# Moving norm steps and tile additions from VectorE to GpSimd in a two-layer transformer kernel

## The chip, the cores and the metric

The kernel runs on one core of a Trainium2 chip. A core has five engines that each work through a queue of their own, in order: TensorE (PE in the profile; PEld is its loading of weights), VectorE (DVE), ScalarE (ACT), GpSimd (POOL) and SyncE (SP), whose queue here carries most DMAs. [...] The metric is the time of one execution on the device in microseconds (us).

## The reference

Two layers share one set of weights. Each is an attention block of 32 heads with 16 numbers per head and a dense block with a ReLU, each behind a layer norm and added back to its input; S = 2048 rows, D = 512, Dff = 1792, all in bfloat16.

```python
def _layernorm(x, axis=-1, eps=1e-5):
    m = jnp.mean(x, axis=axis, keepdims=True)
    v = jnp.var(x, axis=axis, keepdims=True)
    return (x - m) / jnp.sqrt(v + eps)

# _A_ref: q, k, v = x @ wqkv in 32 heads;  softmax(q k^T / 4) v, heads side by side, @ wo
# _B_ref: relu(x @ w1) @ w2
x = A_x
x = x + _A_ref(_layernorm(x), A_wqkv, A_wo)
x = x + _B_ref(_layernorm(x), B_w1, B_w2)
x = x + _A_ref(_layernorm(x), A_wqkv, A_wo)
x = x + _B_ref(_layernorm(x), B_w1, B_w2)
```

## The kernel before

Queries are worked through in chunks of 512 rows (the last chunk of layer 2 in smaller ones). For a head and a block of 128 keys, TensorE makes the scores of 512 queries, 128 x 512, in one bank of PSUM (L2415). Three such blocks make a *slot*. All else hangs on the exponentials of these scores, and two ways of making them run side by side:

- ScalarE takes two or three blocks of a slot in one exp (L2438, 128x1024 or 128x1536).
- The block that is left goes to VectorE (L1798): it adds a bias to the scores and writes int16, which read as bfloat16 is a piecewise exp. Two such blocks, a *pair*, fill one tile ("lin"). GpSimd then makes two more tiles of it, "up" and "down", with `int64_add` (L1867), which adds one constant to four packed int16 at a time. TensorE multiplies all three tiles with V and sums them in PSUM, which averages three piecewise functions.

Of some pairs VectorE adds "lin" and "up" into one tile (L1887, the pair is *joined*), so that TensorE multiplies two tiles instead of three. The products with V go to `ps_f` and `ps_o` (L1441). Everything else (q, k, v, the output product, the dense block) is cut into small groups of matmuls (L482, L753, L744) that fill the gaps of TensorE between two slots.

A norm of a chunk: VectorE takes mean and variance of each 128 rows (L800, L814), ScalarE makes the inverse root by Ln and Exp (L817, L822), VectorE does the last step, subtract the mean and multiply (`ln_apply`, L832), and a transposing DMA on SP's queue turns the 128x512 result into `xnT`, from which the products of TensorE start. Two chunks are turned by TensorE instead (`PLAIN`).

The whole program is written out by a planner in the kernel's Python: it keeps a modelled time for each engine, and decides slot by slot what each engine does next. Constants (`POOL_ADD`, `JOINING`, `APPLY`) and rules (`RULES`, `STARTS`, `JOIN` and so on, keyed by slot number) steer it. What comes out is a fixed order for each engine; the chip decides only how long each waits. `task(...)` puts a step in the queue of `dve`, `pool` or `act`; `joins` decides on a pair; `chain` lays down the steps of a pair.

After the last slot comes a written-out ending (from L2509): the last segment of attention is normalised (`direct`: a lane shuffle, a reciprocal, a multiplication), the output product and the last norm of 128 rows follow, and the last rows of the dense block.

Two lines are of use further down. Near the start (L2001) and right after the last slot (L2509) GpSimd does a small operation whose result nothing uses:

```python
    nc.gpsimd.int64_add(trial, trial, PACKED)                                               # L2001
    nc.gpsimd.tensor_add(out=half_va[0][:], in0=half_ya[0][:], in1=half_ya[0][:])           # L2509
```

Of the kernel before, what the change touches and what calls it, by code (L numbers as in the profile page):

```python
# [26 lines left out]
def kernel(  # L27
# [10 lines left out]
    nc = tc.nc  # L38
# [48 lines left out]
    POOL_TO_DVE, DVE_TO_POOL, SECOND_WAIT = 139.0, 121.0, 76.0  # L87
    APPLY, PORT_END, PORT_LAG, PORT_WON = 324.0, (56.0, 178.0), 117.0, 50.0
# [9 lines left out]
    STARTS, MORE, SLIP, EXTRA, JOIN = {15: 1, 182: 0, 244: 1, 359: 1, 369: 1, 589: 0, 722: 1, 847: 0, 981: 0, 1032: 1, 1209: 0, 1320: 0, 101: 0, 126: 1, 179: 1, 259: 0, 292: 0, 358: 1, 347: 0, 405: 1, 493: 0, 568: 0, 643: 0, 693: 1, 704: 0, 707: 0, 792: 0, 906: 0, 993: 1, 1039: 1, 1097: 1, 1185: 0, 1357: 0, 14: 1, 106: 0, 121: 1, 198: 0, 387: 0, 600: 1, 609: 0, 668: 0, 786: 0, 1035: 0, 1073: 1, 1084: 1, 1219: 1, 1206: 1, 1306: 0, 5: 0, 9: 0, 18: 1, 237: 1, 335: 1, 328: 1, 425: 1, 470: 1, 567: 0, 608: 0, 677: 0, 685: 1, 785: 1, 921: 1, 1098: 0, 1115: 0, 1154: 1, 1182: 0, 1240: 1, 1356: 0}, {31: 1.0, 115: -1.0, 219: 1.0, 236: 2.0, 318: 2.0, 370: 2.0, 393: -1.0, 442: 2.0, 559: 2.0, 615: -1.0, 711: 2.0, 703: -1.0, 736: 1.0, 809: 2.0, 851: 1.0, 1011: 2.0, 1050: -1.0, 1157: 1.0, 1194: -1.0, 1319: 1.0, 188: 2.0, 206: 2.0, 222: -1.0, 239: 1.0, 264: 1.0, 349: 1.0, 469: -1.0, 553: -1.0, 599: -1.0, 635: 1.0, 648: 2.0, 645: -1.0, 657: -1.0, 874: 1.0, 894: -1.0, 909: -1.0, 989: 1.0, 1070: 2.0, 1078: -1.0, 1288: -1.0, 1349: 2.0, 77: 2.0, 79: -1.0, 135: 2.0, 445: 2.0, 476: 2.0, 503: 1.0, 746: -1.0, 805: 1.0, 852: 2.0, 955: -1.0, 982: 2.0, 994: 2.0, 984: 2.0, 1025: -1.0, 1039: 1.0, 1037: -1.0, 1076: 2.0, 1104: 2.0, 1161: -1.0, 1205: 1.0, 1236: 2.0, 1270: 1.0, 1279: 2.0, 1278: 2.0, 1339: -1.0, 6: -1.0, 23: 2.0, 63: 1.0, 99: 2.0, 208: 1.0, 246: 1.0, 389: 1.0, 382: 2.0, 411: 1.0, 438: 1.0, 450: 1.0, 565: -1.0, 608: 2.0, 623: 1.0, 733: 1.0, 766: -1.0, 869: -1.0, 915: 2.0, 1021: -1.0, 1197: 2.0, 1276: 1.0}, {232: 120.0, 318: 60.0, 314: 60.0, 416: 60.0, 550: 120.0, 602: 120.0, 663: -200.0, 810: -200.0, 1018: 120.0, 1083: 60.0, 1099: -200.0, 1185: -200.0, 1222: -200.0, 1248: 216.0, 1273: 60.0, 1292: 60.0, 1300: 120.0, 1335: 216.0, 1337: 120.0, 75: -200.0, 74: 216.0, 100: 120.0, 89: 120.0, 138: 120.0, 137: -200.0, 178: 216.0, 459: -200.0, 683: 60.0, 956: 216.0, 992: 60.0, 1024: 120.0, 1147: 216.0, 1170: -200.0, 1200: -200.0, 1259: 120.0, 14: -200.0, 33: 216.0, 157: -200.0, 209: 60.0, 268: 60.0, 298: 216.0, 349: 60.0, 356: 120.0, 403: 60.0, 411: -200.0, 571: 120.0, 574: -200.0, 664: 60.0, 867: -200.0, 912: 216.0, 905: 216.0, 1184: -200.0, 1188: 60.0, 1228: 120.0, 1269: -200.0, 24: 216.0, 88: -200.0, 111: 60.0, 139: 60.0, 225: 120.0, 224: -200.0, 312: -200.0, 406: 216.0, 616: 216.0, 609: 60.0, 631: 60.0, 625: 216.0, 754: -200.0, 801: 216.0, 857: 120.0, 895: 216.0, 928: -200.0, 976: -200.0, 1060: 120.0, 1075: 120.0, 1114: -200.0, 1128: 120.0, 1162: 60.0, 1168: -200.0, 1217: 60.0, 1227: 216.0, 1330: -200.0}, {92: 2, 166: 1, 249: 1, 286: 2, 328: 1, 395: 1, 398: 1, 478: 1, 491: 1, 519: 1, 615: 1, 716: 1, 737: 2, 785: 2, 881: 2, 989: 2, 991: 2, 1080: 2, 1074: 0, 1202: 0, 1220: 2, 1239: 1, 1264: 1, 1273: 1, 1307: 1, 99: 1, 89: 2, 116: 0, 122: 2, 196: 1, 185: 1, 208: 1, 207: 0, 230: 2, 265: 1, 261: 0, 304: 2, 364: 2, 439: 1, 536: 1, 567: 1, 598: 0, 624: 2, 661: 2, 679: 1, 687: 0, 703: 1, 736: 1, 822: 1, 871: 1, 906: 1, 986: 0, 1036: 1, 1126: 1, 1143: 1, 1151: 1, 1251: 1, 1250: 1, 1336: 1, 1: 1, 21: 2, 40: 0, 70: 1, 88: 1, 138: 0, 146: 0, 337: 2, 340: 2, 356: 0, 394: 0, 443: 1, 480: 1, 495: 1, 485: 1, 604: 0, 613: 0, 627: 2, 633: 0, 659: 1, 676: 1, 697: 0, 689: 2, 717: 0, 754: 1, 782: 1, 795: 0, 902: 1, 987: 0, 1059: 1, 1089: 1, 1100: 2, 1148: 2, 1229: 0, 1303: 0, 1339: 1, 86: 1, 200: 1, 209: 0, 252: 2, 260: 2, 291: 1, 344: 0, 363: 2, 401: 1, 550: 0, 583: 2, 622: 0, 643: 1, 683: 1, 706: 1, 752: 2, 788: 1, 815: 1, 811: 1, 840: 1, 901: 0, 925: 2, 1011: 2, 1116: 0, 1133: 1, 1187: 2, 1222: 0, 1244: 2, 1282: 1, 1346: 1}, {36: 1, 307: 1, 353: 0, 385: 1, 409: 1, 419: 1, 425: 0, 493: 0, 522: 0, 576: 0, 597: 1, 636: 1, 668: 1, 725: 1, 774: 1, 839: 1, 875: 0, 888: 0, 896: 0, 929: 1, 946: 1, 1020: 0, 1042: 0, 1057: 1, 1065: 1, 1144: 0, 114: 0, 162: 1, 234: 0, 302: 1, 330: 1, 372: 0, 386: 0, 630: 0, 623: 1, 748: 1, 770: 0, 871: 1, 1036: 0, 1089: 1, 1205: 0, 1319: 1, 19: 1, 50: 1, 65: 0, 135: 0, 248: 0, 459: 1, 650: 0, 759: 0, 810: 0, 1139: 1, 1142: 1, 37: 0, 390: 0, 451: 1, 457: 1, 492: 1, 500: 0, 523: 0, 554: 0, 648: 0, 733: 0, 736: 1, 744: 0, 805: 1, 827: 0, 999: 0, 1079: 0, 1068: 0, 1111: 1, 1143: 0, 1293: 1, 1341: 1}  # L98
# [6 lines left out]
        "haste": 2.0, "margin": 130.0, "fourth": 1, "lag": 2500.0, "wait": 60.0, "rush": 99.0, "burst": 0.0, "solid": 0, "turn": 0, "urge": 4.0, "debt": 99.0, "group": 1, "swap": 0, "swaplag": 0.0, "join": -1e9, "port": 1e9, "room": 0, "keep": 2, "wide": 1, "share": 4,  # L105
# [30 lines left out]
    qmask = masks[:, 2:4]  # L136
# [170 lines left out]
    def bank():  # L307
        if ending[0]:
            bank_no[0] += 1
            n, now = bank_no[0] % 4, slot[0] % 2  # L310
            in_bank[0] = ((now, 0), (now, 1), (now, 2), (1 - now, 1))[n]
# [50 lines left out]
    def sp_lag(kind, engine="dve", n=1, ask=False):  # L362

        cost, land = kind
        now = (now_pe if engine == "pe" else now_dve)[0]
# [463 lines left out]
    def ln_apply(tag, tt, i, x=None):  # L829
        n = ln_n(tag)  # L830
        xn_waits[0] += i == TPC - 1
        return nc.vector.tensor_scalar(  # L832
            out=xnbuf[i][:], in0=x_t[tt][:] if x is None else x,
            scalar1=mv[n][:, i, 0:1], scalar2=ya_[n][:, i : i + 1],
            op0=ALU.subtract, op1=ALU.mult,
        )
# [18 lines left out]
    def ln_rows(tag, tt, n, i):  # L855
# [1832 lines left out]
```

## Time and profile before

| | |
|---|---|
| three timed runs | 1343.71 us median, 1342.14 to 1346.3 |
| the profiled execution | 1346.03 us, of which the span from first to last instruction is 1344.0 us |
| granted TensorE clock | 0.999 |
| PE busy | 1315.7 us, 98% |
| ACT busy | 1318.8 us, 98% |
| DVE busy | 1233.7 us, 92% |
| POOL busy | 831.3 us, 62% |

A row of the page's groups reads: line, engine, operation, tile written <- tile read, shapes, xcount | busy us, mean ns of one | idle time of the engine just before them in us, and what ended it. "issue" means that the engine waited for nothing that the profile shows. In the timeline a row gives start and length in us, and the idle time before it in square brackets. Buffer numbers are left out of names, so `words` stands for many tiles; freed buffers of other tensors (`ktl`, `val`, `wv`, `xx`) are lent to the pairs and then appear where `words` would.

### The profile page before, as it was taken

The page shows a single profiled execution, that of the slowest core. Times are in us where ns is not written, and L with a number is a line of the kernel's source. Part 1 is how long each engine was busy: PE and PEld are TensorE (multiplying, and loading weights), DVE is VectorE, ACT ScalarE, POOL GpSimd, SP SyncE. Part 2 cuts the span into 40 slices and gives each one's busy share as a digit, 9 for nine tenths or more (in the row PEclk, how much of TensorE's full clock was granted, in tenths as well). Part 3 has the DMA queues.
Part 4 walks back from the last instruction along what each step waited for, and adds up shares of the span by engine and source line. Part 5 has one row for each costly group of instructions (what it writes and reads, how often), then busy time and mean ns, then how long its engine had stood idle before and what let it go on. Part 6 is the DMA issues. An engine that isn't in the chain of part 4 may idle for free.

```text
span 1344.0 us, 48174 instructions
## 1 busy us (share of the span) xinstructions
PE 1315.7 (98%) x20386; PEld 460.3 (34%) x20388; DVE 1233.7 (92%) x2159; ACT 1318.8 (98%) x1417; POOL 831.3 (62%) x1352
## 2 busy tenths in 40 slices
PE   8999999999999999999999999999999999999898
PEld 3322222222222222222232222222234445454666
DVE  8989999999999999988899999999999889999885
ACT  8999999999999999999999999999999999999996
POOL 4358976777567666656556666666556555666541
PEclk9999999999999999999999999999999999999999
DMA  5300112211042120422013100102412413142130
GB/s 146 76 2 19 27 34 57 46 39 33 19 111 55 33 43 18 109 57 42 26 22 99 33 21 6 27 16 50 116 32 48 114 33 74 36 87 56 19 74 20
DMA packets 166344, 66.31 MB, mean 49 GB/s; under 512 B 137552, under 2 KB 161296, under 8 KB 166128
## 3 DMA queue, kind: packets, MB, share of 16 engines
q1 hardware_dynamic: 159600, 57.63, 17.8%
q0 software_dynamic: 5568, 5.15, 2.1%
q8 instruction: 159, 2.61, 0.8%
q10 hardware_dynamic: 960, 0.46, 0.1%
q14 instruction: 57, 0.47, 0.1%
HBM read 38.80 MB, written 4.19 MB: 32 GB/s over the span
## 4 chain that ended last, share of the span: by engine, by line
PE 61%; ACT 31%; DVE 6%; issue 1%; DMA 1%; SPq 0%; POOL 0%; DVEq 0%; ACTq 0%; POOLq 0%
PE ps_s L2415 21%; ACT e L2438 16%; PE ps_f L1441 11%; PE ps_o L482 10%; PE ps_o L1441 9%; PE ps_f L482 7%; ACT xx L2438 4%; ACT w L2438 2%; DVE words L1798 2%; ACT wv L2438 2%; ACT vaug L2438 1%; ACT val L2438 1%; ACT ktp L2438 1%; ACT ktl L2438 1%; PE ps_f L753 1%
## 5 line engine op out<-in xcount | busy, mean ns | idle before, releaser
L2438 ACT ACTIVATE e<-ps_s 128x1024 bf16<-128x1024 f32 (+1 forms) x693 | 767.7, 1193 | 3.1 <-PE ps_s L2415 2.1
L1798 DVE TENSOR_SCALAR words<-ps_s 128x512 int16<-128x512 f32 x815 | 542.2, 682 | 37.8 <-PE ps_s L2415 31.0
L1867 POOL INT64_ADD words<-words x552 | 349.2, 642 | 230.8 <-DVE words L1798 195.6
L2415 PE MATMUL ps_s<-q,ktp 32*128 32x512 bf16 (+2 forms) x4043 | 475.8, 331 | 12.0 <-ACT e L2438 5.7
L2415 PEld LDWEIGHTS <-ktp 32*128 32x128 bf16 x4293 | 150.4, 91 | 452.8 <-issue 446.2
L2438 ACT ACTIVATE xx<-ps_s 128x1024 bf16<-128x1024 f32 x218 | 233.9, 1110 | 3.5 <-PE ps_s L2415 3.2
L2415 PE MATMUL ps_s<-q,ktl 32*128 32x256 bf16 (+2 forms) x1343 | 198.1, 289 | 2.2 <-issue 0.6
L1441 PEld LDWEIGHTS <-vaug 128*32 128x32 bf16 x4566 | 112.7, 95 | 141.8 <-issue 126.9
L1441 PE MATMUL ps_f<-e,vaug 128*32 128x512 bf16 (+2 forms) x873 | 120.4, 335 | 0.6 <-DVE q L1014 0.5
L1441 PE MATMUL ps_o<-e,vaug 128*32 128x512 bf16 (+2 forms) x759 | 111.7, 341 | 0.1
L1798 DVE TENSOR_SCALAR xx<-ps_s 128x512 int16<-128x512 f32 x140 | 93.7, 683 | 12.7 <-PE ps_s L2415 11.0
L1441 PE MATMUL ps_f<-words,vaug 128*32 128x512 bf16 (+1 forms) x576 | 94.0, 366 | 0.3 <-DVE words L1887 0.3
L2438 ACT ACTIVATE w<-ps_s 128x1024 bf16<-128x1024 f32 x85 | 91.1, 1122 | 0.2 <-PE ps_s L2415 0.2
L2438 ACT ACTIVATE vaug<-ps_s 128x1024 bf16<-128x1024 f32 x80 | 86.9, 1132 | 0.9 <-PE ps_s L2415 0.8
L482 PE MATMUL ps_o<-w,ht 128*32 128x512 bf16 x1064 | 84.9, 382 | 0.1
L2415 PEld LDWEIGHTS <-ktl 32*128 32x128 bf16 x1343 | 62.8, 92 | 59.9 <-issue 58.8
L1867 POOL INT64_ADD xx<-words x99 | 62.9, 638 | 30.6 <-DVE words L1798 21.7
L1441 PEld LDWEIGHTS <-val 128*32 128x32 bf16 x2450 | 68.0, 96 | 38.5 <-issue 31.2
L1867 POOL INT64_ADD words<-xx x93 | 58.5, 637 | 34.6 <-DVE xx L1798 31.5
L2438 ACT ACTIVATE wv<-ps_s 128x1024 bf16<-128x1024 f32 x70 | 77.6, 1120 | 0.3 <-PE ps_s L2415 0.3
L1441 PE MATMUL ps_o<-words,vaug 128*32 128x512 bf16 (+1 forms) x445 | 77.7, 372 | 0.0
L1441 PE MATMUL ps_f<-words,vscaled 128*32 128x512 bf16 (+2 forms) x527 | 77.4, 316 | 0.0
(372 smaller groups left out, 2830.5 us busy)
## 6 DMA issues: line engine op xcount, KB each, us to landing
w<-in_B_w_dram SPq DMA_DIRECT2D x144, 128.0 KB
w<-in_B_w_dram SPq DMA_DIRECT2D x35, 256.0 KB
q<-xn SPq DMA_DIRECT2D x34, 64.0 KB
wv<-in_A_wqkv_dram SPq DMA_DIRECT2D x8, 256.0 KB
away<-xx SPq DMA_DIRECT2D x8, 256.0 KB
xx<-away SPq DMA_DIRECT2D x8, 256.0 KB
out_dram<-xx SPq DMA_DIRECT2D x15, 128.0 KB
xx<-in_A_x_dram SPq DMA_DIRECT2D x14, 128.0 KB
```

Source lines behind the costliest of these rows:

```text
L482: nc.tensor.matmul(G["b"][cols], lhsT[:, cols], rhs, start=not G["begun"][g], stop=not G["cols"][g], tile_position=(0, 32 * g), skip_group ...
L753: nc.tensor.matmul(out[cols], lhsT[:, cols], rhs, start=i % k == 0, stop=i % k == k - 1, tile_position=(0, 32 * g), skip_group_check=True,)
L1441: nc.tensor.matmul((ps_f, ps_o)[sg["bank"]][32 * g : 32 * g + 32, 0 : sg["w"]], values[:, 4 * sg["T"] + g, 2 * e : 2 * e + 32], rhs, start ...
L1798: first = nc.vector.tensor_scalar(out=words[which][:, half * QS : (half + 1) * QS], in0=src, scalar1=EXP_BIAS, scalar2=THIRD, op0=ALU.add, ...
L1867: ins = nc.gpsimd.int64_add(of(part).bitcast(I64), of("lin").bitcast(I64), by)
L2415: score = nc.tensor.matmul(b[:, a : a + sg["w"]], kt[32 * g : 32 * g + 32, kc : kc + P], q_home(sg["q"])[32 * g : 32 * g + 32, sg["e"], 0 ...
L2438: ex = nc.scalar.activation(out=eb[:, 0 : place[m]], in_=b[:, 0 : place[m]], func=ACTF.Exp, scale=1.0 / (LOG2E * UNIT),)
```

## The change

1. The last step of every norm that is transposed by DMA is done by GpSimd instead of VectorE (`ln_apply` with `engine=nc.gpsimd`, 55 instructions).
2. A pair can be joined by GpSimd (`by_pool`, a `tensor_tensor` on GpSimd). The decision has a rule of its own (`joinp`) and a third value in the table `JOIN`.
3. In the ending, the reciprocal of the last segment becomes Ln and Exp on ScalarE; the last norm is taken in two halves of 256 columns in two banks, whose last step VectorE and ScalarE do side by side.
4. The planner's tables have some 200 new entries, which shift the order of the work in all slots. ScalarE's exps stay 1347: 127 of 128x1536 (before 141) and 1220 of 128x1024 (before 1206), not counting one of 512. GpSimd has 1275 `int64_add` (before 1261), 59 joins and 55 norm steps.

```diff
+    POOL_APPLY, POOL_JOINING = 800.0, 2250.0
...
-    NORM_UNITS, DIRECT_UNITS, TURN_UNITS = 11.0, 3.0, 1.0
+    NORM_UNITS, DIRECT_UNITS, TURN_UNITS = 9.0, 2.0, 2.0
...
-    def ln_apply(tag, tt, i, x=None):
+    def ln_apply(tag, tt, i, x=None, engine=nc.vector):
         n = ln_n(tag)
         xn_waits[0] += i == TPC - 1
-        return nc.vector.tensor_scalar(
+        return engine.tensor_scalar(
...
             def apply(k):
-                ln_apply(tag, tt + k, k)
                 if not by_dma(tag):
+                    ln_apply(tag, tt + k, k)
                     return
+                ln_apply(tag, tt + k, k, engine=nc.gpsimd)
...
                 task(
-                    APPLY, lambda k=k: apply(k),
+                    POOL_APPLY if by_dma(tag) else APPLY, lambda k=k: apply(k),
...
+        late = now_pool[0] + queued - now_pe[0]
+        long = sg["left"] >= rule["room"]
+        return JOIN.get(slot[0], (
+            2 if late < rule["joinp"] and long
+            else int(early < rule["join"] and late < rule["port"] and long)
         ))
...
         def add():
             x = of("up").bitcast(BF16)
-            ins = nc.vector.tensor_tensor(out=x, in0=x, in1=of("lin").bitcast(BF16), op=ALU.add)
+            engine = nc.gpsimd if p["by_pool"] else nc.vector
+            ins = engine.tensor_tensor(out=x, in0=x, in1=of("lin").bitcast(BF16), op=ALU.add)
...
-        if p["joined"]:
+        if p["joined"] and p["by_pool"]:
+            task(POOL_JOINING, add, [key + ("sum",)], [key + ("up",)], engine="pool")
+            maker[key + ("sum",)].update(chain=p, joins=True)
+        elif p["joined"]:
...
+            def invert():
+                nc.vector.stream_shuffle(out=r[:, 0:width], in_=ps_o[:, 0:width], mask=[lane] * 32)
+                nc.scalar.activation(out=u[:, 0:width], in_=r[:, 0:width], func=ACTF.Ln)
+                nc.scalar.activation(out=u[:, 0:width], in_=u[:, 0:width], func=ACTF.Exp, scale=-1.0)
...
+    uses(
+        nc.vector.tensor_scalar(
+            out=xnbuf[0][:, 0 : D // 2], in0=at_bank(banks[0])[:, 0 : D // 2],
+            scalar1=mv[n][:, 0, 0:1], scalar2=ya, op0=ALU.subtract, op1=ALU.mult,
+        ), banks[0], "x",
+    )
+    uses(
+        nc.scalar.activation(
+            out=xnbuf[1][:, 0 : D // 2], in_=at_bank(banks[1])[:, 0 : D // 2],
+            func=ACTF.Identity, scale=ya, bias=shift,
+        ), banks[1], "x",
+    )
```

How the order of instructions moves is shown at three places. The first is GpSimd's queue near the start, before the change: `int64_add` is named ISA there, with its tiles; a row ISA with no tiles is an instruction that the build puts in by itself. L2001 is the small addition from above, L261 a copy of weights.

```order
L297 MEMSET vaug_15_118 128x16x2
L2000 MEMSET words_150 128x4
L2001 ISA
L2001 ISA words_150<-words_150 128x2
L261 COPY wkq<-w_72 128x16x2x16 x6
L297 MEMSET vaug_0_123 128x16x2
```

From there on GpSimd's 1260 further `int64_add` follow with no bare ISA row among them until L2509, where one stands ahead of the small `tensor_add`. Between GpSimd's operations three bare rows stand in all: ahead of the affine select of masks.py:199, at L2001, and at L2509.

The second place is the same queue of the changed kernel where the first norms follow (L832 is `ln_apply`, `xn` its result; L1884 is the `int64_add` of a pair).

```order
L832 ISA
L832 TENSOR_SCALAR xn_169<-xx_75,mv_176,ya 128x512
L832 TENSOR_SCALAR xn_170<-xx_75,mv_176,ya 128x512
L832 TENSOR_SCALAR xn_171<-xx_76,mv_176,ya 128x512
L832 TENSOR_SCALAR xn_172<-xx_76,mv_176,ya 128x512
L1884 ISA
L1884 ISA words_154<-words_154 128x512
L1884 ISA words_155<-words_154 128x512
L832 ISA
L832 TENSOR_SCALAR xn_169<-xx_77,mv_175,ya 128x512
L832 TENSOR_SCALAR xn_170<-xx_77,mv_175,ya 128x512
L1884 ISA
```

The norm steps have moved here from VectorE's queue, and a bare row stands ahead of each run of them and ahead of the `int64_add` that follows.

The third place is GpSimd's queue of the changed kernel in the middle of layer 1, at a join (L1905).

```order
L1884 ISA words_155<-words_155 128x512
L1884 ISA xx_77<-words_155 128x512
L1905 ISA
L1905 TENSOR_TENSOR words_155<-words_155 128x1024
L1884 ISA
L1884 ISA words_156<-words_151 128x512
L1884 ISA words_154<-words_151 128x512
L1884 ISA xx_79<-words_152 128x512
```

The join has moved here from VectorE, again with a bare row ahead of it and another behind it. Counted over the whole queue there are 59 bare rows ahead of joins, 17 ahead of runs of norm steps (11 runs of four, the others shorter or beside a join) and 76 ahead of the `int64_add` that follows: 152 more than before. By the number of exps that stand ahead of them in the program, 5 of the 76 round trips lie among the first 31 exps, none until exp 167, 62 between exps 167 and 852 (with 55 joins and 28 norm steps), 6 from exp 919 to 1290, and 3 behind exp 1318.

More of the change, by code (lines that the diff above doesn't have):

```diff
@@ L364, in sp_lag @@
         cost, land = kind
-        now = (now_pe if engine == "pe" else now_dve)[0]
+        now = {"pe": now_pe, "dve": now_dve, "pool": now_pool}[engine][0]
         done = max(sp_free[0], now + 200.0) + n * cost
@@ L1316, in direct @@
             def direct(i):
[L1317 removed]
                 if i == 0:
                     nc.vector.stream_shuffle(
[L1320 removed]
+                        out=r[:, 0:width], in_=u[:, 0:width], mask=[lane] * 32
                     )
@@ L2513 @@
     tt, n_rows = chunks[l, j]
-    rows = range(n_rows)
     _, at_column, width = columns(l, j)
@@ L2573, in spare_work @@
         return 0
-    for i in rows:
-        add(banks[i], ident[:], x_t[tt + i][:], True, False)
+    assert n_rows == 1
+    halves = [(banks[0], slice(0, D // 2)), (banks[1], slice(D // 2, D))]
+    first_steps[0]()
+    for b, cols in halves:
+        add(b, ident[:], x_t[tt][:, cols], True, False)
         for T in range(NT // 2):
-            add(banks[i], ot[T][:, part(i)], wo[:, T, :], False, False)
+            add(b, ot[T][:, part(0)], wo[:, T, cols], False, False)
     ending[0] = True
@@ L2587 @@
     spare_work(DIRECT_UNITS)
-    for i in rows:
-        last_steps[0](i)
-        add(banks[i], ot_last[:], wo[:, NT // 2 - 1, :], False, True)
-        if tag not in ln_seq:
-            ln_seq.append(tag)
+    last_steps[0]()
+    for b, cols in halves:
+        add(b, ot_last[:], wo[:, NT // 2 - 1, cols], False, True)
+    if tag not in ln_seq:
+        ln_seq.append(tag)
+    n = ln_n(tag)
+    va, ya = va_[n][:, 0:1], ya_[n][:, 0:1]
+    away_mean, shift = sums[:, 0:1], sums[:, 1:2]
+    for m, (b, cols) in enumerate(halves):
@@ L2593 @@
         uses(
[L2594 removed]
+            nc.vector.bn_stats(out=stats[n][:, m, :], in_=at_bank(b)[:, 0 : D // 2]), b, "x"
         )
[L2596 to L2612 removed]
+    nc.vector.bn_aggr(out=mv[n][:, 0, :], in_=stats[n][:, 0:2, :])
@@ new lines @@
+    uses(
[3 more added lines that the diff above has]
+        ), banks[1], "x",
+    )
+    spare_work(NORM_UNITS)
+    for m, copy in enumerate((nc.vector.tensor_copy, nc.scalar.copy)):
+        pt = at_bank(more[m]).bitcast(BF16)
+        for c in range(NDC // 2):
+            uses(
+                nc.tensor.transpose(
+                    pt[:, c * P : (c + 1) * P], xnbuf[m][:, c * P : (c + 1) * P], ident[:]
+                ), more[m],
+            )
+        of = pt[:, 0 : D // 2].rearrange("p (c f) -> p c f", c=NDC // 2)
+        cs = slice(m * NDC // 2, (m + 1) * NDC // 2)
+        uses(copy(out=xnT[NQS - 1][:, cs, part(0)], in_=of), more[m], "xnT")
@@ L2613 @@
+    for (b, cols), copy in zip(halves, (nc.vector.tensor_copy, nc.scalar.copy)):
+        uses(copy(out=x_t[tt][:, cols], in_=at_bank(b)[:, 0 : D // 2]), b, "x")
     spare_work(sum(c for c, *_ in cur) + TURN_UNITS)
```

68 lines of the change are left out of this document (29 added, 39 removed).

## The prediction

> **What bounds the kernel now.** I read the page's busy shares first, then the groups of ScalarE and GpSimd, then GpSimd's idle time and what ended it.
>
> ```profile
> PE 1315.7 (98%) x20386; PEld 460.3 (34%) x20388; DVE 1233.7 (92%) x2159; ACT 1318.8 (98%) x1417; POOL 831.3 (62%) x1352
> L2438 ACT ACTIVATE e<-ps_s 128x1024 bf16<-128x1024 f32 x561 | 582.5, 1113 | 2.0 <-PE ps_s L2415 1.6
> L2438 ACT ACTIVATE e<-ps_s 128x1536 bf16<-128x1536 f32 x132 | 198.6, 1533 | 1.0 <-PE ps_s L2415 0.5 <-PE ps_o L1441 0.2
> L1867 POOL INT64_ADD words<-words x552 | 349.2, 642 | 230.8 <-DVE words L1798 195.6 <-PE ps_s L2415 22.5 <-PE ps_f L1441 4.5
> ```
>
> ScalarE is the bound: its exps follow each other with 2.0 us of idle time ahead of 561 of them. TensorE is as full. GpSimd is free 38% of the span, and its idle time ends when VectorE has made the next words: it waits for its input and nobody waits for it. A GpSimd that gets more work is harmless only while it stays ahead, so the question is what this change really gives it.
>
> **The price that decides: the bare rows.** Between its operations GpSimd's queue of before has three rows without operands. What stands in the trace at these places:
>
> ```profile
> 0.78 0.20 POOL masks.py:197 MEMSET ident<- 128x128 bf16 x1
> 1.27 0.29 POOL masks.py:199 TENSOR_SCALAR_AFFINE_SELECT ident<-ident 128x128 bf16<-128x128 bf16 x1 [0.29 <-POOL ident masks.py:197]
> 5.49 0.26 POOL L2000 MEMSET words<- 128x4 int16 x1
> 13.12 0.18 POOL L2001 INT64_ADD words<-words  x1 [7.37 <-issue]
> 13.26 4.29 POOL L261 COPY wkq<-w 128x512 bf16<-128x512 bf16 x6
> ...
> 1318.58 1.49 POOL L1867 INT64_ADD words<-words  x2 [0.92 <-DVE words L1798]
> 1327.11 0.18 POOL L2509 TENSOR_TENSOR half_va<-half_ya 128x2 f32<-128x2 f32 x1 [7.04 <-issue]
> ```
>
> The first `int64_add` stands 7.37 us behind the end of the memset ahead of it, waiting for nothing that shows; the `tensor_add` after the last `int64_add` stands 7.04 us behind it, and its input is of the head of the program. Both have a bare row ahead. The copy that follows an `int64_add` without one starts at once. I read a bare row as a switch between two sets of code: one with `int64_add`, one with the tensor operations. The affine select's cost nothing (0.29), which fits a set that is in place when the program starts; that set was called back at L2509 and cost 7.04 all the same, so having been there does not make it cheap. Where both sides alternate, I take 7.37 + 7.04 = 14.4 us for a round trip, and the change makes 76 of them: 76 x 14.4 = 1095 us of GpSimd's time, twice what it has free (1344.0 - 831.3 = 513).
>
> [...]
>
> **What else GpSimd gets.** Neither operation is in its trace with these shapes.
>
> ```profile
> L261 POOL COPY wkq<-w 128x512 bf16<-128x512 bf16 x6 | 4.2, 761 | 0.1
> L832 DVE TENSOR_SCALAR xn<-xx,mv,ya 128x512 bf16<-128x512 bf16 x59 | 25.6, 452 | 0.6 <-ACT ya L822 0.6
> ```
>
> A norm step reads and writes what the copy does: 0.76 us, 55 of them 42 us. A join reads two tiles of 128x1024: at least an `int64_add` (0.64), at most the copy's rate for four times 512 inputs (3.0); I take 2.2, nearer to the copy, 59 of them 130 us. VectorE is rid of 55 x 0.45 = 25 us, which was not on the path.
>
> **How much of it reaches the end.** GpSimd's busy time by stretch, cut where the round trips begin and end (TensorE's, VectorE's and ScalarE's columns stand before GpSimd's):
>
> ```profile
> 0.00:31.00 31.00, 27.55 (x291) 10.43 (x295) 26.58 (x63) 26.69 (x37) 13.82 (x45) 1.00 0.60 154
> 31.00:166.00 135.00, 132.48 (x1606) 37.78 (x1603) 127.83 (x222) 135.00 (x143) 90.56 (x150) 1.00 0.14 32
> 166.00:853.00 687.00, 678.69 (x8522) 190.52 (x8518) 641.54 (x1081) 682.59 (x733) 449.83 (x717) 1.00 0.19 44
> 853.00:1318.00 465.00, 454.63 (x9539) 205.25 (x9533) 425.45 (x766) 460.85 (x485) 275.42 (x438) 1.00 0.25 57
> 1318.00:1344.00 26.00, 22.35 (x449) 16.28 (x447) 12.33 (x32) 13.64 (x25) 1.67 (x3) 1.00 0.07 19
> ```
>
> There are 1347 exps in 1344 us, one per microsecond, so exps 167 to 852 are the stretch of 687 us. 62 of the 76 trips lie there.
>
> - Least, if GpSimd never idles there: 449.8 + 62 x 14.4 + 55 x 2.2 + 28 x 0.76 = 1485 us, that is +798. (With joins at 0.64 it is +712, at 3.0 +842.)
> - Most, if nothing of a trip is hidden: 62 x 14.4 = +893. The joins and norm steps (142) fit into the 237 us that GpSimd has free there.
>
> Between these decides how far GpSimd is ahead of TensorE, since TensorE runs its queue in order and stops at the first product that needs a late tile; then scores stop, and ScalarE and VectorE with them. A tile that can be followed by its name:
>
> ```profile
> L1441 PE MATMUL ps_o<-ktl,vaug x6: 378/379/380, 37.9 to 38.6; 128*32 128x512 bf16 x6
> L1867 POOL INT64_ADD ktl<-words x1: 611/611/611, 34.3 to 34.3; - x1
> ```
>
> Made from 34.3 to 34.9, read from 37.9: 3.0 us ahead. So of each trip about 3 us are hidden, and TensorE then stands for some 10 us. That has a price of its own. After standing, as at the start of the program, its matmuls are slow:
>
> ```profile
> 1.18 5.20 PE L1904 MATMUL ps_o<-e 128*128 128x512 bf16 x12 [1.18 <-DVE e L268]
> 1318.69 0.82 PE L482 MATMUL ps_f<-w,ht 128*32 128x512 bf16 x12
> ```
>
> At the start twelve follow each other in 5.20 us, 0.43 each; later twelve, four side by side, take 0.82, that is 0.27 a round. For some 5 us TensorE has about half its rate. It is nearly full otherwise, so that is worth up to 2.5 us a trip; in the middle of the trace it never stands long enough to show it, so the bounds are 0 and 2.5, and I take 2.0, nearer to the only row there is. [...]
>
> Per trip of the stretch: planned 687 / 62 = 11.1 us, + 14.4, - 3.0, + 2.0 = 24.5 us, just over the 24.0 that GpSimd's own work takes. 62 x 24.5 - 687 = **+832**.
>
> The rest: 5 trips at the start, 72 us, of which up to 10 may find GpSimd idle anyway (**+67**); 6 trips between 853 and 1318, 86 us, less up to 3.6 each (**+75**); 3 at the end, 43 us, less up to 11 (**+38**). The tensor operation after the very last `int64_add` stands there before and after and is not counted. GpSimd serves transposes too: a late norm step delays SP's transposing DMAs and the products behind them, but by the same trip, so I add nothing.
>
> **What the change gains otherwise.** 14 exps have 1024 columns instead of 1536: 14 x (1533 - 1113) ns = 5.9 us of the bound engine. The ending's chain of waits goes through these:
>
> ```profile
> 1327.75 0.95 DVE L1323 RECIPROCAL u<-u 128x128 f32<-128x128 f32 x1
> 1329.64 0.70 DVE L2594 BATCH_NORM_STATS2 stats<-ps_s 128x6 f32<-128x512 f32 x1 [0.55 <-PE ps_s L2530]
> 1331.15 0.81 DVE L832 TENSOR_SCALAR xn<-ps_s,mv,ya 128x512 bf16<-128x512 f32 x1 [0.60 <-ACT ya L822]
> 1330.59 0.29 ACT L817 ACTIVATE va<-mv,masks 128x1 f32<-128x1 f32 x1 [1.40 <-DVE mv L814]
> ```
>
> Two ScalarE steps like the last (0.29 each, and two hand-overs) for 0.95 gain nothing or 0.3; the last step in two halves side by side gains about 0.4; the statistics in halves nothing. Together -0.7 us, bounds 0 and -1.5. It is a hundredth of what the trips cost.
>
> **Sum**, against the profiled execution's own 1346.0 (span 1344.0 and 2.0 around it, 2.3 above the median): 1346.0 - 5.9 - 0.7 + 832 + 67 + 75 + 38 = 2351; on the median's scale 2349. **Forecast: 2350 us, slower by 1000.** Its own range is 2200 (joins at 0.64, GpSimd saturated) to 2480 (nothing hidden: 1339 + 893 + 72 + 86 + 43 = 2433, and some of the slow TensorE).
>
> **Rivals.**
>
> - *One direction is cheap.* The 7.37 was the first load of that code, with transfers under way, and a set once loaded comes back for nothing. Against: the other set had been in place and took 7.04. If only the way to `int64_add` is cheap, a trip costs 7.2: the stretch is 62 x max(11.1 + 7.2 - 3.0 + 2.0, 16.8) - 687 = +386, the rest (5 + 6 + 3) x 5 = +70: about 1795 us.
> - *Nothing is hidden and TensorE is slow each time.* 2433 + 76 x 2.5 = 2623 us. For it: norm steps come in runs between two `int64_add` of one pair, where no lead has been built up. Against: GpSimd waits for VectorE, not the other way round, nearly everywhere.
> - *The bare rows cost nothing where they are common* (the other side). The mechanism: the 7 us gaps belong to the first call of an operation in a program, not to the row. The affine select's 0.29 speaks for it. Then the change does what its text says, GpSimd has 831 + 172 us of work in 1344, and ScalarE's 5.9 and the ending's 0.7 come through: 1343.7 - 6.6 = 1337 us, faster. It decides from a switch under about 1.5 us, where the lead of 3.0 us covers a trip.
>
> **Chances.** Forecast 0.79; one direction cheap 0.08; nothing hidden 0.07; the rows cost nothing 0.06. The range that should hold the time 8 times in 10 is 2180 to 2500: the forecast's own, with room for switches of 6.5 us (76 x 1.4 = 106 less) below and for the slow TensorE above. A measurement of this kernel tells 0.3% from no change. Only the last case is not slower: faster 0.05, within 0.3% 0.01, slower 0.94.
>
> **What would show it.** GpSimd's groups of the norm step and the join have some 7.0 us of idle time by "issue" ahead of each run, and so have the `int64_add` behind them: some 1100 us by "issue" on GpSimd in all. ScalarE's and TensorE's busy time in us stays near 1315 while their shares fall to 55 to 60%. The slices between a twelfth and two thirds of the old program are stretched to about twice, and those between exps 31 and 166, where no trip lies, keep their 135 us. TensorE waits for GpSimd's tiles, which it never did. The granted clock falls below 1.0 in the stretched slices if standing costs the clock. I am wrong if a switch in the middle costs much less than 7 us, or if GpSimd's idle time remains large in the stretch, which would mean that its input is what comes late.

## The result and the profile after

The changed kernel takes 2401.77 us (median of 6 runs, 2399.99 to 2404.32), the kernel before 1344.09 us beside it (6 runs, 1342.14 to 1346.3). The ratio is 1.787, with an interval of 1.785 to 1.789: 1058 us more. The profiled execution has a span of 2399.8 us.

The page of the changed kernel, its busy shares and two rows of its forty slices:

```profile
PE 1529.0 (64%) x20316; PEld 479.0 (20%) x20317; DVE 1249.5 (52%) x2111; ACT 1350.0 (56%) x1422; POOL 1075.4 (45%) x1480
...
PE   6199656654564665656365555466576988897856
...
PEclk8599777786776787776677676667788998898987
```

No engine is full any more. ScalarE, the bound of before, works 1350 us of 2400, and TensorE 64% of the span, at a granted clock that is below full speed in most slices. GpSimd, which got the work, counts as busy for 45%. A reader who looks for the engine with the highest share finds none. The time is in the idle column of the groups:

```profile
L2459 ACT ACTIVATE e<-ps_s 128x1024 bf16<-128x1024 f32 (+1 forms) x726 | 783.2, 1130 | 649.1 <-PE ps_s L2436 593.5
...
L1884 POOL INT64_ADD words<-words x551 | 344.8, 634 | 363.6 <-issue 184.1
...
L832 POOL TENSOR_SCALAR xn<-xx,mv,ya 128x512 bf16<-128x512 bf16 x55 | 113.9, 2075 | 122.7 <-issue 36.0
...
L1905 POOL TENSOR_TENSOR words<-words,words 128x1024 bf16<-128x1024 bf16 x22 | 46.8, 2128 | 157.6 <-issue 121.5
```

ScalarE's `e` exps have 649 us of idle time ahead of them where there were 3, nine tenths of it ended by scores from TensorE. Why TensorE is late stands in its waits, and why GpSimd is late in its own (columns: us in total, times, the longest):

```profile
PE ps_o L1454 <- POOL words L1884: 140.0, 31, 16.4
PE ps_o L1454 <- POOL words L1905: 108.7, 15, 29.7
PE ps_f L1454 <- POOL words L1884: 106.8, 13, 18.2
```

```profile
POOL words L1884 <- issue: 255.5, 43, 6.2
POOL words L1905 <- issue: 201.8, 28, 8.2
...
POOL xn L832 <- issue: 36.0, 5, 7.6
```

TensorE stops at products with V whose tile GpSimd has not made yet. Before, none of its waits was for GpSimd. GpSimd is late by "issue", time in which it waits for nothing that the profile shows, and, but for a few us at the program's start and end, in one kind of place only: 255.5 / 43 = 5.9 us ahead of an `int64_add` that follows a join or a norm step, 201.8 / 28 = 7.2 us ahead of a join and 36.0 / 5 = 7.2 us ahead of a norm step that follow an `int64_add`. Two such trips in GpSimd's timeline (start, length, idle time ahead in brackets):

```profile
722.51 2.10 POOL L1905 TENSOR_TENSOR w<-w,words 128x1024 bf16<-128x1024 bf16 x1 [8.14 <-issue]
730.91 0.60 POOL L1884 INT64_ADD xx<-words  x1 [6.29 <-issue]
...
746.20 2.10 POOL L1905 TENSOR_TENSOR words<-words,words 128x1024 bf16<-128x1024 bf16 x1 [7.10 <-issue]
754.10 1.79 POOL L1884 INT64_ADD words<-words  x3 [5.80 <-issue]
```

For 2.1 us of addition GpSimd is away from its `int64_add` for 15 to 17 us, and for a good part of that VectorE, ScalarE and TensorE stand: of the two absences, 16.6 and 15.0 us, TensorE works for 4.0 and 4.6 us, VectorE for 4.6 and 5.5, ScalarE for 4.5 and 5.5.

Where the time went, by the same exps: both spans are cut where exps 61, 167, 853 and about 1346 start, and only ScalarE's exps are counted (stretch, its length, busy time and number of exps, granted clock, DMA share, GB/s). Before:

```profile
0.00:77.50 77.50, 66.44 (x60) 1.00 0.39 96
77.50:176.80 99.30, 98.83 (x107) 1.00 0.08 16
176.80:836.30 659.50, 655.40 (x687) 1.00 0.19 46
836.30:1322.90 486.60, 482.00 (x494) 1.00 0.24 54
1322.90:1344.00 21.10, 3.28 (x4) 1.00 0.07 21
```

After:

```profile
0.00:152.70 152.70, 66.14 (x60) 0.74 0.19 49
152.70:252.50 99.80, 98.76 (x107) 1.00 0.08 16
252.50:1736.20 1483.70, 679.36 (x687) 0.73 0.08 20
1736.20:2364.00 627.80, 486.23 (x493) 0.89 0.18 42
2364.00:2399.80 35.80, 3.44 (x4) 0.81 0.04 13
```

The second row is the clearest. There GpSimd does neither a join nor a norm step, and 107 exps take 99.8 us where they took 99.3, at full clock, between two stretches that are twice and more as long as before. The five differences are +75.2, +0.5, +824.2, +141.2 and +14.7 us, 1055.8 in all.

### The profile page after: what moved, and what is told of

Read it like the earlier page. It is cut to its first block, busy times and chain, and to the rows that moved or that the text cites. A ratio compares the mean times of both kernels' runs of the same rounds, so it can differ in the third digit from the quotient of the medians.

```text
span 2399.8 us, 48252 instructions
## 1 busy us (share of the span) xinstructions
PE 1529.0 (64%) x20316; PEld 479.0 (20%) x20317; DVE 1249.5 (52%) x2111; ACT 1350.0 (56%) x1422; POOL 1075.4 (45%) x1480
## 2 busy tenths in 40 slices
DMA packets 166346, 66.33 MB, mean 28 GB/s; under 512 B 137552, under 2 KB 161296, under 8 KB 166128
## 5 line engine op out<-in xcount | busy, mean ns | idle before, releaser
L2436 PE MATMUL ps_s<-q,ktp 32*128 32x512 bf16 (+2 forms) x4053 | 527.0, 361 | 92.0 <-DVE words L1811 48.6
L1884 POOL INT64_ADD words<-words x551 | 344.8, 634 | 363.6 <-issue 184.1
L1454 PE MATMUL ps_o<-words,vaug 128*32 128x512 bf16 (+1 forms) x536 | 113.5, 425 | 124.8 <-POOL words L1905 70.2
L832 POOL TENSOR_SCALAR xn<-xx,mv,ya 128x512 bf16<-128x512 bf16 x55 | 113.9, 2075 | 122.7 <-issue 36.0
L1454 PE MATMUL ps_o<-e,vaug 128*32 128x512 bf16 (+2 forms) x1003 | 154.8, 367 | 1.4 <-DVE ht L1274 0.8
L1905 DVE TENSOR_TENSOR words<-words,words 128x1024 bf16<-128x1024 bf16 x62 | 51.9, 838 | 188.2 <-POOL words L1884 188.2
L1454 PE MATMUL ps_o<-words,val 128*32 128x256 bf16 (+2 forms) x649 | 78.6, 315 | 108.0 <-POOL words L1884 68.2
L1454 PE MATMUL ps_f<-words,vaug 128*32 128x512 bf16 (+2 forms) x401 | 76.5, 406 | 74.0 <-POOL words L1884 43.3
L1905 POOL TENSOR_TENSOR words<-words,words 128x1024 bf16<-128x1024 bf16 x22 | 46.8, 2128 | 157.6 <-issue 121.5
L1454 PE MATMUL ps_o<-xx,vaug 128*32 128x512 bf16 (+1 forms) x343 | 85.2, 434 | 47.8 <-POOL xx L1905 19.2
L1884 POOL INT64_ADD xx<-words x125 | 78.9, 633 | 76.8 <-issue 47.5
L1454 PE MATMUL ps_o<-words,vscaled 128*32 128x512 bf16 (+2 forms) x564 | 108.0, 362 | 3.3 <-POOL words L1884 3.0
```

Source lines behind the costliest of these rows:

```text
L832: return engine.tensor_scalar(out=xnbuf[i][:], in0=x_t[tt][:] if x is None else x, scalar1=mv[n][:, i, 0:1], scalar2=ya_[n][:, i : i + 1], ...
L1454: nc.tensor.matmul((ps_f, ps_o)[sg["bank"]][32 * g : 32 * g + 32, 0 : sg["w"]], values[:, 4 * sg["T"] + g, 2 * e : 2 * e + 32], rhs, start ...
L1884: ins = nc.gpsimd.int64_add(of(part).bitcast(I64), of("lin").bitcast(I64), by)
L1905: ins = engine.tensor_tensor(out=x, in0=x, in1=of("lin").bitcast(BF16), op=ALU.add)
L2436: score = nc.tensor.matmul(b[:, a : a + sg["w"]], kt[32 * g : 32 * g + 32, kc : kc + P], q_home(sg["q"])[32 * g : 32 * g + 32, sg["e"], 0 ...
```

## The experiments

Two theories stood after the result. **Switching**: each time GpSimd goes from `int64_add` to a tensor operation or back it stands for 6 to 7 us, and TensorE, in order, stands with it. **Work**: the joins and norm steps themselves, or the new order of all slots, make GpSimd or another engine late. Below, the kernel before ran beside each group of runs; its median was 1344.92 us for the first four, 1344.35 for the next four and 1343.58 for the last.

### All of it back on VectorE, in the changed order

```diff
-                ln_apply(tag, tt + k, k, engine=nc.gpsimd)
+                ln_apply(tag, tt + k, k)
...
-            engine = nc.gpsimd if p["by_pool"] else nc.vector
+            engine = nc.vector
```

> The changed kernel with its plan, its tables and its new ending, but the 55 norm steps and 59 joins are issued to VectorE again, at the same places of the program; GpSimd then switches its code three times, as before the change. If the round trips of GpSimd are the cause: 1335 to 1365 us (the 59 joins bring some 45 us of VectorE work back into an engine that is 92% busy). If the new plan or ending is at fault: over 1450 us.

Measured: 1369.43 us, ratio 1.019 (1.017 to 1.021). The granted clock is 0.996.

```profile
PE 1331.1 (97%) x20316; PEld 460.7 (34%) x20317; DVE 1270.8 (93%) x2225; ACT 1326.6 (97%) x1422; POOL 856.6 (63%) x1366
```

114 instructions change their engine, and 1032 of the 1058 us are gone. So the new order and the new ending are not what costs. 25 us remain, somewhat more than was expected: the exps fall behind those of before gradually, 2 us by exp 60, 21 by exp 852, 25 at the end, while VectorE has 37 us more work than before (1270.8 against 1233.7). Most of that are joins which the kernel before does not make: it joins 127 pairs (L1887), the changed order 180 (L1905), and of these the changed kernel leaves 121 to VectorE and gives 59 to GpSimd. So most of GpSimd's joins are new work, not work taken from VectorE.

### One part at a time

The joins alone on GpSimd, norm steps on VectorE:

```diff
-                ln_apply(tag, tt + k, k, engine=nc.gpsimd)
+                ln_apply(tag, tt + k, k)
```

> The changed kernel with the norm steps on VectorE; the 59 joins stay on GpSimd (59 round trips of the 76). Cost by the number of trips (13.3 us each in the stretch with 62 of them): about 1340 + 59 x 13.3 = 2125 us, 2050 to 2180. Cost by GpSimd's longer work instead of its switches (59 joins of 2.1 us): under 1500 us.

The norm steps alone on GpSimd, joins on VectorE:

```diff
-            engine = nc.gpsimd if p["by_pool"] else nc.vector
+            engine = nc.vector
```

> The changed kernel with the joins on VectorE; the 55 norm steps stay on GpSimd (17 round trips). By trips: 17 x (12.7 of switches + 4 to 5 for norm steps that take 2.07 instead of the planned 0.8 - 3 of lead + 2 of slow TensorE) = 17 x 16 = 272: about 1610 us, 1560 to 1660. If the slow clock of TensorE feeds on itself rather than following each trip, more than 1700 us.

Measured: 2117.51 us for the joins (ratio 1.575, 1.572 to 1.578), 1663.66 us for the norm steps (1.237, 1.234 to 1.240). The joins came out as expected, the norm steps just above the range. Both expectations start from about 1340 us, where the same order without trips takes 1369, and the second counts 17 trips, where there are 18; with both put right its 16 us a trip give 1657. 59 joins cost 773 us and 55 norm steps 319, though a norm step takes as long as a join (2.08 and 2.13 us in the groups above). What differs is the number of trips: the planner puts up to four norm steps behind each other. GpSimd's timeline of the second kernel:

```profile
26.73 8.28 POOL L832 TENSOR_SCALAR xn<-xx,mv,ya 128x512 bf16<-128x512 bf16 x4 [6.88 <-DVE stats L800]
41.29 1.20 POOL L1884 INT64_ADD words<-words  x2 [6.27 <-issue]
```

Four steps share one trip there, 8.28 us of work between 6.88 and 6.27 of standing. In all the 55 norm steps make 18 trips (one of the runs stood beside a join, which made it part of that join's trip) and the 59 joins make 59, so a trip costs 319 / 18 = 17.7 and 773 / 59 = 13.1 us. Against the run with all of it on VectorE (1369.4), which has the same order, it is 294 / 18 = 16.3 and 748 / 59 = 12.7; these two losses add up to 1042 us, where both together lose 1032. The trips with norm steps are longer by their work, and most of this work is not hidden.

### The same amount of work without switches

Each norm step and join of GpSimd becomes a copy by GpSimd of a tile of the same shape; the arithmetic of these steps is left out. GpSimd's timeline of before had shown that a copy follows an `int64_add` at once (at 13.26 us, with no idle time ahead of it).

```diff
+        if engine is nc.gpsimd:
+            return engine.tensor_copy(out=xnbuf[i][:], in_=x_t[tt][:])
...
+            if p["by_pool"]:
+                ins = engine.tensor_copy(out=x, in_=of("lin").bitcast(BF16))
```

> The changed kernel with each norm step and each join of GpSimd replaced by a copy on GpSimd of the same shape (the norm's arithmetic and the addition of these joins are left out, so its output is another); a copy needs no switch of code, so GpSimd keeps its order, its waits and most of its work. If the switches are the cause: 1330 to 1350 us, what the change was to bring. If handing this work to GpSimd is the cause, whatever code it needs: over 1700 us.

Measured: 1348.91 us, ratio 1.004 (1.003 to 1.006).

```profile
PE 1314.0 (98%) x20316; PEld 459.4 (34%) x20317; DVE 1227.8 (91%) x2111; ACT 1317.3 (98%) x1422; POOL 925.4 (69%) x1480
```

```profile
L833 POOL COPY xn<-xx 128x512 bf16<-128x512 bf16 x55 | 31.7, 612 | 0.4 <-DVE w L1813 0.4
```

As many instructions stand in the same places on GpSimd (1480, as in the changed kernel), and the loss is gone. A copy is shorter than what it stands for (0.61 us instead of 2.08), so this run alone takes two things away, the switches and 150 us of work (1075.4 - 925.4). The copies also don't read the inverse root, and some start up to 0.6 us before it is there. With 925 us of 1347 GpSimd would have room for the 150. The run says one thing more: even without switches the changed kernel is 4 us slower than before, not 6.6 faster.

### The switch by itself

To the kernel before is added, behind every 60th `int64_add`, an addition of two columns that nothing reads:

```diff
+            added[0] += 1
+            if added[0] % 60 == 0:
+                nc.gpsimd.tensor_add(out=spare_in[:, 0:2], in0=spare_in[:, 2:4], in1=spare_in[:, 2:4])
```

> The kernel before with one more instruction behind every 60th int64_add of GpSimd: a tensor_add of 128x2 floats that nothing reads (0.2 us by itself). That is 21 round trips and nothing else. If a trip costs what it takes (12.7 us in the changed kernel's trace) less some 3 us of lead plus some 2 of slow TensorE: 1344 + 21 x 11.7 = 1590 us, 1540 to 1640. If only the first call of an operation is dear: under 1360 us.

Measured: 1578.12 us, ratio 1.174 (1.172 to 1.176), as expected. The 21st addition stands behind the very last `int64_add`, where GpSimd switched before as well, so 20 trips cost 234 us: 11.7 each, for 20 x 0.18 = 4 us of work. The group of the added line:

```profile
L1874 POOLq MODIFY_POOL_CONFIG  x42: 4/11/21, 102.2 to 1552.1; - x42
```

This is the bare row of the prediction. It has a name in the trace, where it leaves two records each time (42 for the 21 ways to the addition; in the changed kernel 118 ahead of joins, 34 ahead of norm steps and 152 ahead of the `int64_add` that follows, 304 for its 152 rows), and takes 11 ns itself (the median); the 6 to 7 us (7.10 and 5.80 at the trip below) come after it and belong to no row. What GpSimd does in them no run shows, nor the two sets of code that the prediction reads into the row; the changed kernel's DMA queues move 66.33 MB in all, those of before 66.31. What one trip does to the rest: first GpSimd's timeline, then TensorE's.

```profile
575.73 0.18 POOL L1874 TENSOR_TENSOR spare_in<-spare_in 128x2 f32<-128x2 f32 x1 [7.10 <-DVE val L992]
581.72 0.60 POOL L1870 INT64_ADD words<-words  x1 [5.80 <-issue]
```

```profile
582.38 0.61 PE L1443 MATMUL ps_f<-words,vaug 128*32 128x512 bf16 x2 [3.88 <-POOL words L1870]
...
586.47 0.58 PE L2421 MATMUL ps_s<-q,ktp 32*128 32x512 bf16 x1 [2.95 <-DVE w L1801]
```

The same in slices of 4 us (stretch, length, then busy time of TensorE, its weight loads, VectorE, ScalarE and GpSimd, granted clock, DMA share, GB/s):

```profile
574.00:578.00 4.00, 4.00 (x55) 1.09 (x55) 2.74 (x5) 4.00 (x5) 0.18 (x1) 1.00 0.02 4
578.00:582.00 4.00, 0.49 (x6) 0.00 (x0) 0.00 (x0) 1.20 (x2) 0.28 (x1) 0.78 0.00 0
582.00:586.00 4.00, 1.15 (x4) 0.20 (x4) 1.28 (x2) 1.02 (x1) 4.00 (x7) 0.50 0.00 0
586.00:590.00 4.00, 3.53 (x23) 0.49 (x22) 2.90 (x5) 1.02 (x1) 3.25 (x6) 0.50 0.00 0
590.00:594.00 4.00, 4.00 (x53) 1.11 (x54) 3.65 (x6) 3.59 (x4) 2.00 (x4) 0.94 0.10 33
594.00:598.00 4.00, 4.00 (x56) 1.02 (x56) 3.77 (x8) 4.00 (x6) 2.95 (x6) 1.00 0.13 41
```

GpSimd is away from 568.6 to 581.7. Until 578.5 nobody notices. Then TensorE stops for 3.88 us, VectorE as well, and the clock falls to a half; the first scores after that wait for VectorE, which has only now begun again, for another 2.95. TensorE comes back at 0.50: in the slice that ends at 590 it does 23 matmuls in 3.53 us, in the next 53 in 4.00. Of the twelve us from 578 to 590 ScalarE, the bound, works 3.2. Not every place is alike: by the starts of the same exps in this trace and in that of before, the 20 trips cost from 6.5 to 14.3 us each, this one 9.4.

### One trip

The same addition once, behind the 600th `int64_add` (`== 600` for `% 60 == 0`).

> The same with a single round trip, behind the 600th int64_add. By the trip's price 1344 + 11.7 = 1356 us, 1352 to 1361. If GpSimd's idle time of 38% takes a single trip in: 1344 to 1346 us.

Measured: 1351.14 us (1348.64 to 1353.69), ratio 1.0059 (1.0043 to 1.0074). That is 6.8 us and between the two expectations: a single trip costs, though about half of the mean of the twenty. It is the place that is cheap, since the tenth of the twenty trips stands at the same one. The first product that has to wait there, in the run with 20 trips and in this one:

```profile
728.25 0.58 PE L1443 MATMUL ps_f<-words,vaug 128*32 128x512 bf16 x1 [3.45 <-POOL words L1870]
```

```profile
622.44 0.58 PE L1443 MATMUL ps_f<-words,vaug 128*32 128x512 bf16 x1 [3.49 <-POOL words L1870]
```

In both TensorE works on for 10.2 us after GpSimd has left, stops for 3.5, and held against the kernel before, the exps behind the trip have fallen back by 6.0 and 6.2 us. A trip has no fixed price: at this place, where TensorE finds tiles for 10.2 us, it costs 6.0 to 6.8 us, and 11.7 on average over the twenty.

### GpSimd away without a switch

At the same 21 places GpSimd does 80 tiny `int64_add` instead of the addition.

```diff
+                for _ in range(80):
+                    nc.gpsimd.int64_add(spare_in[:, 4:8].bitcast(I64), spare_in[:, 0:4].bitcast(I64), PACKED)
```

> The kernel before with 80 tiny int64_adds of one number each at the same 21 places where e5_trips21 has its tensor_add: GpSimd is away for some 10 to 15 us (the profile will say how long) without a switch. If a trip costs only by GpSimd's absence, the added time per place is that length less about 1 us, as in e5_trips21. If the switch does harm beyond it (to the other engines' memory or transfers), e9_away is cheaper by a fifth or more at the same length.

Measured: 1778.35 us, ratio 1.323 (1.321 to 1.326). The 80 took longer than was expected, one absence in GpSimd's timeline:

```profile
164.32 1.20 POOL L1870 INT64_ADD val<-words  x2
165.49 22.66 POOL L1875 INT64_ADD spare_in<-spare_in  x80
188.13 0.61 POOL L1870 INT64_ADD words<-xx  x1
```

So the run missed its number and still answers its question. With 20 places that count, 434 / 20 = 21.7 us are lost at each, for an absence of 22.7. No bare row stands at these places, and the loss relates to the absence as it does at the trips. All runs in one table; an absence is the two waits of a trip by the rows of the changed kernel (5.9 + 7.2 = 13.1) and the work done in it (59 joins of 2.11 us, 55 norm steps of 2.08, shared among the trips), the last column is TensorE's busy time over that of before (1315.7), per trip:

| run | trips | away, us | lost per trip, us | difference | TensorE busy more, us |
|---|---|---|---|---|---|
| 20 trips with nothing in them | 20 | 13.3 | 11.7 | 1.6 | 2.9 |
| absence without a switch | 20 | 22.7 | 21.7 | 1.0 | 2.8 |
| joins alone | 59 | 15.2 | 13.1 | 2.1 | 3.2 |
| norm steps alone | 18 | 19.5 | 17.7 | 1.8 | 2.5 |
| the change | 76 | 16.2 | 13.9 | 2.3 | 2.8 |

The last three rows have the order of the changed kernel. Against the run with all of it on VectorE (1369.4 us, TensorE busy for 1331.1) they lose 12.7, 16.3 and 13.6 us a trip, the differences are 2.5, 3.2 and 2.6, and TensorE is busy for 2.9, 1.7 and 2.6 us more.

Whatever GpSimd does while it is away, in these five runs all but 1 to 3 us of it are lost on average. A switch shows no other harm in them than its length. The first two rows are the cleanest, being the same 20 places: by the traces the absences are 9.4 us longer without the switch, and 10.0 us more are lost at each.

The small difference has large parts. In the run with 20 trips TensorE works on for 3.4 to 10.2 us after GpSimd has left until its first stop for a late tile or score, 6.6 on average, and at the same places of the run without a switch for the same times within 0.3. Then it stands: by the traces' spans 8.7 us a trip more than in the kernel before, which is 1.9 more than the 13.4 - 6.6 = 6.8 that are left of the absence, as in the trip above, where the scores had to wait for VectorE to start again. And its work takes 2.9 us longer: 8.7 + 2.9 = 11.6. So the 12.7 - 3 + 2 = 11.7 that was expected of a trip is right by luck: more is hidden than 3, and the start after it costs more than 2.

### The new ending alone

The kernel before, with its tables, and the ending of the changed kernel (Ln and Exp for the reciprocal, the last norm in two halves).

```diff
-            nc.vector.bn_stats(out=stats[ln_n(tag)][:, i, :], in_=at_bank(banks[i])), banks[i], "x"
+            nc.vector.bn_stats(out=stats[n][:, m, :], in_=at_bank(b)[:, 0 : D // 2]), b, "x"
```

> The kernel before with the changed ending alone (Ln and Exp for the reciprocal, the last norm in two halves on two engines, its unit constants), and the tables of before. The prediction put the ending at -0.7 us with bounds 0 and -1.5: 1343.0 to 1344.5 us, hardly to be told from no change. If the ending is what the change lives of: under 1341 us.

Measured: 1343.31 us (11 runs), ratio 0.9993 (0.9984 to 1.0002). No change that can be told, as expected.

### Planned anew for VectorE

Here the planner knows that VectorE does all joins and norm steps, and places them anew; table and ending are the changed ones.

```diff
-            how = joins(taken[0][0])
+            how = min(joins(taken[0][0]), 1)
...
-                    POOL_APPLY if by_dma(tag) else APPLY, lambda k=k: apply(k),
+                    APPLY, lambda k=k: apply(k),
```

> The changed kernel with every norm step and join on VectorE, as in the run with 1369, but here the planner knows it: it counts these steps on VectorE and no longer chooses pairs for GpSimd, so words, joins and norm steps are placed anew; the new table and the new ending stay. If the 25 us that the first run of this kind lost come from a plan made for a GpSimd that helps, this one returns to the kernel before: 1335 to 1350 us. If the new table itself is worse, 1355 to 1375. If the narrower exps of the new table are worth what the prediction took (5.9 us, and 0.7 for the ending), 1337 us.

Measured: 1385.96 us (5 runs), ratio 1.032 (1.030 to 1.034), slower than with the plan left alone and above all three expectations.

```profile
PE 1330.0 (96%) x20245; PEld 474.0 (34%) x20246; DVE 1226.8 (89%) x2131; ACT 1346.3 (97%) x1423; POOL 799.0 (58%) x1294
```

The planner relieves VectorE by handing exps back to ScalarE: 195 exps are 128x1536 where before had 141, GpSimd has 1203 `int64_add` where it had 1261, and ScalarE 1346.3 us of work where it had 1318.8, 27.5 us more on the engine that is the bound. The rest of the 42 us was not followed up. So the new table does not pay without GpSimd's help, and GpSimd's help does not pay with it; no kernel tried here beats the one before by more than can be told.

## Why the prediction was right

It forecast 2350 us (2180 to 2500), slower, and the kernel takes 2402. What costs, and that it costs once per trip, was right; that the sum comes out so near is in part luck, since its terms were off both ways. By its steps:

- **The bare rows.** Right in kind: a wait stands behind each of the 152 that the change adds, the tensor operations do not come back for nothing, and there are 76 trips. The size was a little off: the way to the tensor operations has 7.2 us (taken: 7.04), the way back to `int64_add` 5.9 (taken: 7.37, from the first use at the head of the program), 13.1 a trip instead of 14.4.
- **The stretch from exp 167 to 852.** Forecast +832, measured +824. Per trip that is 13.4 and 13.3, nearly the same number, made of parts that were each off and cancel, which is luck. The switches are 1.3 us a trip shorter. Of lead and slow TensorE, 3.0 - 2.0 = 1.0 was to be hidden, and 2.6 are (13.1 of switches and 2.8 of work, less the 13.3); the 3.0 of lead, read from one tile, is 6.6 on average in the run with 20 trips, and that TensorE stands 1.9 us longer than the tiles are late was not in the sum. Against this stood the step that failed: "The joins and norm steps (142) fit into the 237 us that GpSimd has free there." They do not go there. The work is done while GpSimd is away already and TensorE waits or is about to, and lengthens the absence: empty trips cost 11.7 us, the joins alone 12.7 to 13.1 a trip, that is 1.0 to 1.4 more for the 2.1 of a join; trips with norm steps cost 4.6 to 6.0 more for 6.4 us of steps (the lower figures against the run with all of it on VectorE). These stand at other places than the empty trips; at equal places 9.4 us more of absence cost 10.0. The free time lies in other places.
- **The norm step.** Taken as the copy's 0.76 us, since it reads and writes as much; it takes 2.08, as long as a join of two tiles of twice the length. The copy stayed a copy's length (0.61 in the run with copies). 55 x 1.3 = 72 us too little, and mostly not hidden.
- **The other pieces.** Start: +67 forecast, +75 measured. Exps 853 on and the end: +75 and +38 forecast, 141.2 + 14.7 = 156 measured. Behind exp 852 lie 15 norm steps and 5 joins, 15 x 2.08 + 5 x 2.11 = 42 us, which were counted at nothing; 113 + 42 = 155. That this fits so well is luck too: the switches there are shorter than forecast, and by time one trip more lies there, the one at exp 853. At the start lie 12 norm steps, 25 us, of which the same sum would take too much (92): there GpSimd has little else to do.
- **Exps 31 to 166 keep their time.** From exp 32 on they do, 131.5 us to exp 167 where before had 129.4; the fifth trip stands between exps 31 and 32, and not ahead of them.
- **Slow TensorE.** Taken as 2.0 us a trip from the only row at the program's start, and a drop of the clock was left open. TensorE's busy time, which was to stay near 1315 us, is 1529.0: 213 / 76 = 2.8 us a trip. The trace of before could have told, against the reading that TensorE "never stands long enough to show it": it has one stop of 1.77 us in its middle, behind a late transposing DMA, and a granted clock of 0.50 for 3.4 us from there (the rows stand in the last section). The clock does fall after standing: to 0.50 in the slices behind the trip that is shown above, where TensorE stood for 3.88 us, and to 0.50 behind the stop of 1.77 us of before.
- **Idle time by "issue" on GpSimd, some 1100 us.** 76 x 13.1 = 996; added up one by one in the trace the 152 waits are 1004 us. The view puts 763 of them down to "issue" and the rest to other engines.
- **What the change gains otherwise.** 6.6 us forecast, from narrower exps and the ending. The ending gave nothing that can be told (0.9993). The narrower exps don't show either: in the run with copies ScalarE is busy for 1317.3 us, 1.5 less than before and not 5.9, and the kernel is 4 us slower. By the same exps of the two profiled executions it is 1.4 us ahead at exp 1200 and 1.5 behind at the last, and its ending is 1.5 us longer; which of its waits grew was not settled.
- **Relief of VectorE**, costed at nothing because it was not on the path. In the order of the changed kernel it seems to be: with the 114 steps on VectorE that kernel takes 1369.4 us, with copies in their place on GpSimd 1348.9, for 43 us less work of VectorE. The order of before, with 53 joins less, gets the same time without this relief.

Of the rivals, "one direction is cheap" falls with the 5.9 and 7.2 us in the rows, and "nothing is hidden" with 11.7 lost of 13.3, and 6.8 of 13.0 at the single trip. "The bare rows cost nothing where they are common" falls with the 20 empty trips.

## What to carry to other kernels

Idle time by "issue" after a row that belongs to no operation is a price to be counted, and here it recurs at every alternation, 7.2 us on the way to a join or norm step and 5.9 on the way back: a trip for 0.2 us of work costs about 12 us, so operations with such a row ahead of them belong on another engine, or in a few groups that share one trip, as four norm steps did. An engine's free time, here 38% of the span, was not free for work that is on the way of a queue that runs in order: what counted is how far ahead its tiles are at that place, here 3 to 10 us, and what an absence exceeded this was lost, with some 5 us more for the start after it (1.9 of standing and 2.9 of slow work). Two shares to look at when all engines fall to 50 or 60%: the idle column, and the clock.

## What the runs showed of the hardware

The TensorE clock is the surprise. In the changed kernel its mean over the span is:

```profile
core 0: 2399.8 us, clock 0.785
```

If it is either full or half, it was at half for (1 - 0.785) / 0.5 x 2399.8 = 1032 us, an estimate, although TensorE stands for less: 871 us of the span without a matmul in all. By the clock's own records in the trace, which hold 1.00 and 0.50 alone, it is 1034 us at half, and TensorE works in 428 of them; half of these is 214, and 213 is what it is busy more than before. So the slow work is the clock. The trip shown above, cut where the clock changes (columns as there):

```profile
578.49:580.28 1.79, 0.00 (x0) 0.00 (x0) 0.00 (x0) 0.71 (x1) 0.00 (x0) 1.00 0.00 0
580.28:590.52 10.24, 5.20 (x35) 0.94 (x38) 4.55 (x7) 2.44 (x3) 7.54 (x12) 0.50 0.00 0
```

The clock fell 1.8 us after TensorE's last matmul and stayed at half for 10.2 us, in which TensorE worked for 5.2. The kernel before shows the same once, behind a stop of 1.77 us; TensorE's timeline, then the stretch behind the stop:

```profile
637.65 1.47 PE L482 MATMUL ps_o<-xnT,wkq 128*32 128x512 bf16 x12 [1.77 <-DMA xnT<-xn]
```

```profile
637.60:641.00 3.40, 3.35 (x26) 0.70 (x26) 1.09 (x3) 1.02 (x1) 0.40 (x1) 0.50 0.02 5
```

And the norm step, a tensor operation with one tile and two columns of scalars, took GpSimd 2.08 us for 128x512 in the changed kernel, over three times a copy of the same tile (0.61 in the run with copies), and as much as the sum of two tiles of 128x1024 (2.11).
